# Router logits as plain float32 products on four column groups, scale tables right behind the token indices, and one filter unit moved out of the head

## The chip, the cores and the metric

The kernel is one launch on one core of a Trainium2 chip. A core has TensorE (matrix products and transposes), VectorE, ScalarE, GpSimd and SyncE (which issues most DMAs); the profile calls them PE, DVE, ACT, POOL and SP, and PE's loading of stationary operands is listed apart as PEld. The metric is device time in microseconds (us), the median of three runs.

## The reference

The output is `x + A(xn) + B(xn)` with `x = A_q` (2048 tokens x 512 channels, float32) and `xn` its layer norm.

- `A`: a 4-tap causal filter of `A_k` over time, times `A_v`; then a causal convolution over all 2048 steps with one filter per channel (`A_ssm_k`), plus a skip term `A_ssm_D`, times `xn`.
- `B`: a mixture of experts. `logits = xn @ w_gate` (512 x 8); each token takes its two best experts; the gates are the softmax of the two logits; expert e computes `silu(xn @ w1[e]) @ w2[e]` (512 to 1792 to 512), and the weighted results are summed.

```python
logits = xf @ w_gate
topk_idx = jnp.argsort(-logits, axis=-1)[:, :K]
topk_val = jnp.take_along_axis(logits, topk_idx, axis=-1)
gates = _softmax(topk_val, axis=-1)
```

## The kernel before

Products that must be exact use float32 values cut into a rounded part (a 4-byte format that TensorE reads in one pass, `F32R`) and a low part, in three products: rounded by rounded, rounded by low, low by rounded. A plain float32 product takes two passes, and the trace has two records for it.

The **head** runs before the first expert. `load_x` loads the tokens (eight tiles, 16 rows of tokens per partition in all), a table of constants and the filters `ks`. `logits` takes the tokens in four chunks of 512. For each chunk and each of four slices of 128 channels (`dc`) TensorE transposes four blocks into a PSUM tile `pt` (L253), ScalarE writes the rounded part `xTh` (L254), VectorE the low part `xTl` (L255). Eight products with the 16 columns of `wgr` (8 rounded, 8 low columns of the gate weights less their mean) add up in `pl` (L259). ScalarE copies `pl` to `lt` (L262), four small transposes bring it token by token into `pb` (L265), and VectorE adds the two halves to `lgt` (L271, L272). The mean and variance of the tokens (`stats`, L280) are put between, held back by explicit order.

`routing` finds each token's two best experts on VectorE (L353 to L365), counts tokens per expert and gives every token its place by products with triangular tables (L369 to L374), ranks the experts by load, and builds for the largest expert a one-hot table `tabA` (L552). Sixteen products with it (L433) give the list of that expert's tokens; VectorE turns it into indices `gix` (L580), and GpSimd gathers the tokens with six indirect DMAs (L885). `perm`, the experts in order of load, tells SyncE which weights to load (L974, L937). Another sixteen products with the same table (L571) give each gathered token its two scale values for the layer norm; `scales` copies them (L473), and VectorE normalizes the gathered tokens (L924). They are transposed (L905), cut into `xh` and `xl` (L909, L910), and the first expert's products start (L963): first those of the first three blocks of tokens (`u` = 0), then those of the other three.

**Filter units.** The long convolution goes through a two-step transform; its first step on the filters is `conv_k(pair, q8)`, eight units. A unit is eight transposes (L708), a copy by ScalarE (`kt`, L711), four float32 products of 512 columns, two on each half of TensorE's rows (L645), four copies from PSUM (L653, in one unit two of them on VectorE, L651) and two writes to DRAM (L673). PSUM has four banks for these products, the same four that the transposes of tokens use. Five units, (0,0) to (0,3) and (1,0), run in the head, as filling for TensorE; three run as background work between the first expert's products, as all other work on the convolution does between those of the experts.

The order on each engine comes from a list scheduler; `self.after(late, early, ...)` binds one instruction behind another, and `step` puts a unit's transposes or products behind the last instruction of its chain, `gate_t`. Six products of no use (`pads`, L428) stand ahead of the list.

## Time and profile before

| | us |
|---|---|
| median of three runs | 866.47 |
| lowest, highest | 865.88, 872.0 |
| the profiled execution | 868.49 |
| its span, first to last instruction | 866.7 |
| TensorE busy in the span | 837.3 |

The profiled execution takes 1.8 us more than its span, and 2.0 us more than the median. The profile gives, for each engine, its busy time; a table by stretches of the span with the granted share of TensorE's clock (1.00 is 2.4 GHz, 0.50 is 1.2 GHz); a list of instructions in order of time, in which neighbours of the same line are merged; and groups of instructions with their mean durations. Records of TensorE overlap, since a product starts before the one ahead has left the array.

### The profile page before, as it was taken

How to read it: one execution, taken by the hardware profiler on the slowest of the kernel's cores; microseconds unless marked ns; L12 is line 12 of the kernel's file. 1: busy time of each engine (PE TensorE's matmuls, PEld its weight loads, DVE VectorE, ACT ScalarE, POOL GpSimd, SP SyncE). 2: the span in 40 equal slices, each digit the busy share in tenths (PEclk: the TensorE clock that was granted, in tenths of full speed). 3: DMA queues.
4: the chain of work that ended last, by engine and by line, in shares of the span. 5: the costliest groups of instructions: out<-in, count | busy, mean ns of one | idle time of the engine just before them, and what ended most of it. 6: DMA issues, size and time to landing. Idle time of an engine off the chain costs nothing. (4 is left out here: it accounts for less than half of the span.)

```text
span 866.7 us, 13867 instructions
## 1 busy us (share of the span) xinstructions
PE 837.3 (97%) x5052; PEld 733.4 (85%) x5052; DVE 598.7 (69%) x878; ACT 499.3 (58%) x783; POOL 173.9 (20%) x168
## 2 busy tenths in 40 slices
PE   9889999999999989999999899999999989999996
PEld 7569998998998989998999788887888868888885
DVE  6869754679888746577766688658766489985421
ACT  4567425355433555567776678557875479654420
POOL 0110022460403402033020160105001220003231
PEclk9999999999999999999999999999999999999999
DMA  9599749969999675667465676656744599877971
GB/s 343 183 290 357 276 128 269 259 199 233 232 274 250 189 221 168 192 195 214 152 210 183 203 229 200 184 180 231 238 151 144 170 327 286 248 232 229 273 205 66
DMA packets 147506, 190.98 MB, mean 220 GB/s; under 512 B 12785, under 2 KB 106347, under 8 KB 146860
## 3 DMA queue, kind: packets, MB, share of 16 engines
q1 hardware_dynamic: 131356, 147.29, 56.7%
q0 software_dynamic: 16080, 42.78, 17.0%
q8 instruction: 41, 0.67, 0.3%
q14 instruction: 29, 0.24, 0.1%
HBM read 143.88 MB, written 50.63 MB: 224 GB/s over the span
## 5 line engine op out<-in xcount | busy, mean ns | idle before, releaser
L950 DVE TENSOR_TENSOR wl<-wraw,wh 128x1024 fp32r<-128x1024 f32 (+1 forms) x116 | 137.5, 1185 | 115.4 <-ACT wh L947 99.4
L947 ACT ACTIVATE wh<-wraw 128x1024 fp32r<-128x1024 f32 (+1 forms) x116 | 119.4, 1029 | 154.8 <-PE ps L963 103.4
L963 PE MATMUL ps<-xh,wh 128*128 128x512 f32 (+4 forms) x672 | 184.8, 327 | 9.9 <-ACT ht L1001 6.9
L963 PE MATMUL ps<-xl,wh 128*128 128x512 f32 (+4 forms) x672 | 184.0, 325 | 0.0
L963 PE MATMUL ps<-xh,wl 128*128 128x512 f32 (+4 forms) x672 | 183.3, 324 | 0.0
L963 PE MATMUL ps<-h,wh 128*128 128x288 f32 (+3 forms) x896 | 154.8, 292 | 2.5 <-ACT ht L1001 2.5
L963 PEld LDWEIGHTS ps<-xh,wh 128*128 128x128 f32 x672 | 113.6, 189 | 25.7 <-ACT ht L1001 10.0
L963 PEld LDWEIGHTS ps<-h,wh 128*128 128x128 f32 x896 | 129.5, 190 | 6.8 <-issue 3.0
L963 PEld LDWEIGHTS ps<-xl,wh 128*128 128x128 f32 x672 | 114.1, 189 | 9.8 <-issue 0.8
L963 PEld LDWEIGHTS ps<-xh,wl 128*128 128x128 f32 x672 | 114.1, 189 | 9.2
L1000 ACT ACTIVATE h<-ps 128x512 fp32r<-128x512 f32 (+4 forms) x112 | 67.9, 606 | 56.7 <-PE ps L963 56.5
L1002 DVE TENSOR_TENSOR h<-ht,h 128x512 fp32r<-128x512 f32 (+4 forms) x112 | 78.5, 705 | 27.2 <-ACT ht L1001 25.7
L963 PE MATMUL ps<-h,wl 128*128 128x288 f32 (+3 forms) x448 | 95.3, 292 | 0.0
L1032 POOL DMA_INDIRECT acc_d<-acc,ids x36 | 48.6, 1351 | 195.4 <-DVE acc L1029 187.5
L1051 PE MATMUL py<-wl,h 128*128 128x512 f32 x224 | 87.7, 391 | 0.0
L1052 PE MATMUL py<-wh,h 128*128 128x512 f32 x224 | 87.5, 391 | 0.0
L1050 PE MATMUL py<-wh,h 128*128 128x512 f32 x224 | 86.8, 391 | 0.0
L963 PEld LDWEIGHTS ps<-h,wl 128*128 128x128 f32 x448 | 72.0, 191 | 1.9 <-issue 1.5
L1001 ACT ACTIVATE ht<-ps 128x512 f32<-128x512 f32 (+4 forms) x112 | 68.1, 610 | 1.3 <-PE pty L1096 1.3
L1016 POOL DMA_INDIRECT acc<-acc_d,gix x36 | 46.7, 1297 | 86.9 <-PE ptx L905 52.1
L885 POOL DMA_INDIRECT xg<-xn_d,gix x34 | 39.7, 1167 | 114.2 <-DVE tb L581 55.4
L814 DVE TENSOR_TENSOR ka<-pu,ka 128x512 f32<-128x512 f32 x32 | 22.1, 692 | 40.8 <-ACT ka L808 37.1
(238 smaller groups left out, 1226.0 us busy)
## 6 DMA issues: line engine op xcount, KB each, us to landing
wraw<-in_B_w_dram SPq DMA_DIRECT2D x84, 512.0 KB
wraw<-in_B_w_dram SPq DMA_DIRECT2D x32, 448.0 KB
zk_d<-ev SPq DMA_DIRECT2D x16, 512.0 KB
zv_d<-ev SPq DMA_DIRECT2D x16, 512.0 KB
mid<-in_c_mid_dram POOLq DMA_DIRECT2D x16, 512.0 KB
z<-zk_d SPq DMA_DIRECT2D x32, 256.0 KB
z<-zv_d SPq DMA_DIRECT2D x32, 256.0 KB
zi_d<-zo SPq DMA_DIRECT2D x32, 256.0 KB
```

The costliest lines, as they stand in the source:

```text
L885: self.gather = nc.gpsimd.indirect_dma_start(out=t[:sb], out_offset=None, in_=self.xn_d[:, :] if r else self.io["A_q"].rearrange("o s d -> ...
L947: w = nc.scalar.activation(hi, raw, AF.Copy)
L950: t = nc.vector.tensor_sub(lo, raw, hi)
L963: self.mm = nc.tensor.matmul(ps[:, u, :n], w, x[:, u, :], start=first and w is wh and k == 0, stop=last and w is wl)
L1000: nc.scalar.activation(h, ps[:, :nu, :n], AF.Silu)
L1001: acts.append(nc.scalar.activation(t, ps[:, :nu, :n], AF.Silu))
L1002: self.hid = nc.vector.tensor_sub(l, t, h)
L1016: nc.gpsimd.indirect_dma_start(out=acc[:sb], out_offset=None, in_=sum_d[:, :], in_offset=bass.IndirectOffsetOnAxis(ap=self.gix[:sb, c0 + b ...
L1032: st = nc.gpsimd.indirect_dma_start(out=sum_d[:, :], out_offset=bass.IndirectOffsetOnAxis(ap=self.ids[:sb, c0 + b:c0 + b + 1], axis=0), in ...
L1050: nc.tensor.matmul(o, a, wh[:, f, :], start=ff == 0, stop=False)
L1051: nc.tensor.matmul(o, a, wl[:, f, :], start=False, stop=False)
L1052: nc.tensor.matmul(o, l, wh[:, f, :], start=False, stop=ff == FC - 1)
```

## The change

- **Logits.** The transposed tokens stay float32 (`xT`), with one copy by ScalarE; `xTl` and VectorE's subtractions are gone. Each slice of 128 channels has its own group of 32 of the array's columns (`pl[dc * Q:...]`, L257), with the gate weights padded to 32 columns by zeros: four float32 products per chunk, each into its own 32 partitions of `pl`, none added to another. ScalarE copies all 128 partitions to `lt` (L259), and a product with `pick`, a 0/1 matrix, adds the four groups and turns the result token by token into `pb` (L262). VectorE reads the logits straight from PSUM.
- **Statistics.** They follow each chunk, and the reciprocal deviations with them; on VectorE all 16 stand ahead of the first maximum (L343), and the steps from variance to the cut scales too. The load of ScalarE's table for SiLU moves behind the logits.
- **Routing.** The products of the scale tables (L558) stand right behind the list's (L423), their operands ahead of the indices on VectorE; `perm` and the copy of the places (`pos`) come behind the indices instead of ahead.
- **Units.** Four in the head, (0,0) to (0,3); (1,0) joins the background work of the first expert. All copies of the head's units are on ScalarE. The loads of both filter pairs are issued at the start, with a part of the constant table (`rc`) and of the transform (`ev`) between them.

```diff
         nc.sync.dma_start(rt, io["c_rt"][:, :cut])
-        nc.sync.dma_start(rc, io["c_rt"][:, cut:])
+        self.dv = self.cp.tile([P, DC], F32, name="dv")
+        nc.sync.dma_start(self.dv, io["A_ssm_D"].rearrange("(c p) -> p c", p=P))
...
+        self.ks = [self.load_k(cp, 0)]
         nc.sync.dma_start(self.ev, io["c_edge"][:, :P])
+        nc.sync.dma_start(rc, io["c_rt"][:, cut:])
+        self.ks.append(self.load_k(cp, 1))
...
-        wc = sp.tile([P, DC, E], F32, name="wc")
-        wg = sp.tile([P, DC, 2, E], F32R, name="wgr")
+        wc = sp.tile([P, DC, Q], F32, name="wc")
+        nc.gpsimd.memset(wc, 0.0)
         for dc in range(DC):
-            V.tensor_sub(wc[:, dc, :], self.wg[:, dc, :], pb[:, 1, :E])
-        V.tensor_copy(wg[:, :, 0, :], wc)
-        V.tensor_sub(wg[:, :, 1, :], wc, wg[:, :, 0, :])
-        self.L = sp.tile([P, NI, E], F32, name="lgt")
-        lp = sp.tile([P, NI, E], F32, name="lgp", tag="tmp")
+            V.tensor_sub(wc[:, dc, :E], self.wg[:, dc, :], pb[:, 1, :E])
+        pick = sp.tile([P, E], F32, name="pick")
+        V.tensor_reduce(pick, self.ident.rearrange("p (g q) -> p q g", q=Q)[:, :E, :], axis=AX.X, op=ALU.add)
...
         for c in range(4):
             x = self.x[4 * c:4 * c + 4]
-            xh = bp.tile([P, DC, D], F32R, tag="big", name="xTh")
...
+            xt = bp.tile([P, DC, D], F32, tag="big", name="xT")
             for dc in range(DC):
...
-                evict = nc.scalar.activation(xh[:, dc, :], pt, AF.Copy)
-                self.low[c, dc] = V.tensor_sub(xl[dc], pt, xh[:, dc, :])
+                nc.scalar.activation(xt[:, dc, :], pt, AF.Copy)
             pl = self.pmm.tile([P, 2, D], F32, tag="mm", name="pl")
-            for k, xt in enumerate(([xh[:, dc, :] for dc in range(DC)], xl)):
-                for dc in range(DC):
-                    nc.tensor.matmul(pl[:2 * E, 0, :], wg[:, dc].rearrange("p a e -> p (a e)"), xt[dc],
-                                     start=k == 0 and dc == 0, stop=k == 1 and dc == DC - 1)
...
-            lt = cp.tile([P, 4, DH], F32, tag="b4", name="lt")[:2 * E].rearrange("p a b -> p (a b)")[:, :D]
-            evict = nc.scalar.activation(lt, pl[:2 * E, 0, :], AF.Copy)
+            for dc in range(DC):
+                nc.tensor.matmul(pl[dc * Q:(dc + 1) * Q, 0, :], wc[:, dc, :], xt[:, dc, :], start=True, stop=True)
+            lt = cp.tile([P, 4, DH], F32, tag="b4", name="lt").rearrange("p a b -> p (a b)")[:, :D]
+            self.evict = nc.scalar.activation(lt, pl[:, 0, :], AF.Copy)
...
-                nc.tensor.transpose(pb[:, 0, 2 * jj * E:2 * (jj + 1) * E], lt[:, j * P:(j + 1) * P],
-                                    self.ident[:2 * E, :2 * E])
-            if c == 2:
-                self.stats(0)
-                self.stats(1)
-        pv = pb[:, 0, :2 * NI * E].rearrange("p (j a e) -> p j a e", j=NI, a=2)
-        V.tensor_copy(lp, pv[:, :, 1, :])
-        V.tensor_add(self.L, pv[:, :, 0, :], lp)
-        self.evict = evict
-        self.stats(2)
+                nc.tensor.matmul(pb[:, 0, jj * E:(jj + 1) * E], lt[:, j * P:(j + 1) * P], pick, start=True, stop=True)
+            self.stats(c)
+        self.L = pb[:, 0, :NI * E].rearrange("p (j e) -> p j e", j=NI)
+        self.rstds(sp)
...
-        self.stats(3)
         rs = sp.tile([P, 2, NI], F32, name="rs")
-        self.after(V.tensor_scalar_add(rs[:, 0, :], mv[:, :, 1], 1e-5), self.ranked, "the routing comes first")
-        self.rooted = nc.scalar.activation(self.rstd, rs[:, 0, :], AF.Sqrt)
-        self.after(self.rooted, self.evict, "the logits come first")
-        self.after(V.reciprocal(self.rstd, self.rstd), self.indexed, "the routing comes first")
+        V.tensor_scalar_add(rs[:, 0, :], mv[:, :, 1], 1e-5)
...
+        t = nc.scalar.activation(self.warm, self.warm, AF.Silu)
+        self.after(t, rooted, "the square root comes first")
+        self.after(t, self.evict, "the logits come first")
+        self.silu = t
...
+        step((0, 1))
+        step((0, 0))
         step((0, 2), held=self.held)
-        step((0, 1))
-        step((0, 3), held=self.held)
...
-        self.listed = self.gate_t = t
-        step((0, 2))
-        step((1, 0), shared=True, held=self.held)
-        step((0, 3))
-        self.ev03 = self.evicted
...
-        pv = sp.tile([1, E], F32, name="pv")
-        w9 = sp.tile([1, E, E], F32, name="w9")
-        V.tensor_mul(w9, ro[:1].rearrange("p e r -> p r e"), b1(rt["e0"])[:1])
-        V.tensor_reduce(pv, w9, axis=AX.X, op=ALU.add)
-        V.tensor_copy(self.perm, pv)
-        pos = t3("pos")
-        self.after(V.tensor_copy(pos.rearrange("p j e -> p (j e)"), pp[:, :P]), self.rtid, "the table comes first")
-
         tid0 = sp.tile([P, NBLK[0]], F32, name="tid0")
         self.indexed = self.unpack_tid(pt0, tid0[w], 0, NBLK[0], w)
         self.gathers(0)
-        self.rstds(sp)
+        pv = sp.tile([1, E], F32, name="pv")
+        w9 = sp.tile([1, E, E], F32, name="w9")
+        self.after(V.tensor_mul(w9, ro[:1].rearrange("p e r -> p r e"), b1(rt["e0"])[:1]), self.indexed,
+                   "the indices come first")
+        V.tensor_reduce(pv, w9, axis=AX.X, op=ALU.add)
+        ranks = V.tensor_copy(self.perm, pv)
+        pos = t3("pos")
+        self.after(V.tensor_copy(pos.rearrange("p j e -> p (j e)"), pp[:, :P]), ranks, "the ranks come first")
...
-        done = self.products(A0, B0, R1, parts, pt1, self.gate_t)
+        self.products(A0, B0, R1, parts, pt1, self.listed)
+        self.gate_t = self.tabled
+        step((0, 1))
+        step((0, 3), held=self.held)
+        step((0, 2))
+        self.ev02 = self.evicted
+        step((0, 3))
...
-        self.gate_t = self.tabled
-        step((1, 0))
...
-        if q8 == 0:
-            self.ks = self.load_k(cp, pair)
-        ks = self.ks
+        ks = self.ks[pair]
...
-            for q8 in range(2):
-                self.heads[0, q8] = self.conv_k(cp, 0, q8, True)
-                next(self.heads[0, q8])
-            for _ in self.heads[0, 0]:
-                pass
+            self.heads[0, 0] = self.conv_k(cp, 0, 0, True)
+            next(self.heads[0, 0])
...
-            units += [("k", lambda q8=q8: self.conv_k(cp, 1, q8)) for q8 in (1, 2, 3)]
+            units += [("k", lambda q8=q8: self.conv_k(cp, 1, q8)) for q8 in range(4)]
```

Three places in TensorE's own list of instructions, before and now (every row is an instruction or a run of equal ones; x16 is sixteen). Line numbers are those of the two files.

The first chunk of logits. Before:

```order
L253 MATMUL pt<-ident,x 128x128 x16
L259 MATMUL pl<-xTh,wgr 16x512 x2
L253 MATMUL pt<-ident,x 128x128 x4
L259 MATMUL pl<-xTh,wgr 16x512
L253 MATMUL pt<-ident,x 128x128 x4
L259 MATMUL pl<-xTh,wgr 16x512
L259 MATMUL pl<-xTl,wgr 16x512 x3
L253 MATMUL pt<-ident,x 128x128 x4
L259 MATMUL pl<-xTl,wgr 16x512
L253 MATMUL pt<-ident,x 128x128 x12
```

Now:

```order
L253 MATMUL pt<-ident,x 128x128 x16
L257 MATMUL pl<-xT,wc 32x512
L253 MATMUL pt<-ident,x 128x128 x4
L257 MATMUL pl<-xT,wc 32x512
L253 MATMUL pt<-ident,x 128x128 x4
L257 MATMUL pl<-xT,wc 32x512
L253 MATMUL pt<-ident,x 128x128 x4
L257 MATMUL pl<-xT,wc 32x512
L253 MATMUL pt<-ident,x 128x128 x16
L262 MATMUL pb<-pick,lt 128x8 x4
```

Four runs of the second chunk's transposes stood between eight products before; now they stand between four, so that each of the first chunk's products has transposes on both sides, where later chunks have four in a row.

From the last logits to the counts (`sel` marks the chosen experts, `ks` the filters). Before:

```order
L265 MATMUL pb<-ident,lt 128x16 x4
L708 MATMUL ptk<-ident,ks 128x128 x16
L645 MATMUL ps_397<-kt,ev 128x512
L645 MATMUL ps_396<-kt,ev 128x512
L645 MATMUL ps_403<-kt,ev 128x512
L645 MATMUL ps_402<-kt,ev 128x512
L369 MATMUL pw<-rt,sel 128x128
L372 MATMUL pw<-sel,rt 128x128
L373 MATMUL pw<-rt,cs 128x128
L374 MATMUL pw<-rt,cs 128x8
```

Now:

```order
L262 MATMUL pb<-pick,lt 128x8 x4
L690 MATMUL ptk<-ident,ks 128x128 x8
L359 MATMUL pw<-rt,sel 128x128
L362 MATMUL pw<-sel,rt 128x128
L363 MATMUL pw<-rt,cs 128x128
L364 MATMUL pw<-rt,cs 128x8
L690 MATMUL ptk<-ident,ks 128x128 x8
```

Eight transposes and the four products of unit (0,0) stood between the last logits and the first product that needs `sel`; now there are eight transposes alone, and (0,0)'s products come behind the counts.

The list, the scale tables (`tabR` with 24 columns) and the units. Before:

```order
L428 MATMUL pw<-ones 128x128 x6
L433 MATMUL pw<-tabR,tabA 96x6 x16
L645 MATMUL ps_538<-kt,ev 128x512
L645 MATMUL ps_537<-kt,ev 128x512
L645 MATMUL ps_544<-kt,ev 128x512
L645 MATMUL ps_543<-kt,ev 128x512
L708 MATMUL ptk<-ident,ks 128x128 x8
L645 MATMUL ps_570<-kt,ev 128x512
L645 MATMUL ps_569<-kt,ev 128x512
L645 MATMUL ps_576<-kt,ev 128x512
L645 MATMUL ps_575<-kt,ev 128x512
L571 MATMUL pw<-tabR_638,tabA 96x24 x16
```

Now:

```order
L418 MATMUL pw<-ones 128x128 x6
L423 MATMUL pw<-tabR,tabA 96x6 x16
L558 MATMUL pw<-tabR_524,tabA 96x24 x16
L632 MATMUL ps_548<-kt,ev 128x512
L632 MATMUL ps_547<-kt,ev 128x512
L632 MATMUL ps_554<-kt,ev 128x512
L632 MATMUL ps_553<-kt,ev 128x512
L690 MATMUL ptk<-ident,ks 128x128 x8
L632 MATMUL ps_575<-kt,ev 128x512
L632 MATMUL ps_574<-kt,ev 128x512
L632 MATMUL ps_581<-kt,ev 128x512
L632 MATMUL ps_580<-kt,ev 128x512
```

The scale tables' sixteen products moved from behind two units to right behind the list's. Behind the rows shown follow one more unit's four products and the transposes of the gathered tokens.

## Rows read from the trace of the kernel before

**Rows 1.** The page: the span; busy time of an engine, its share of the span, its instructions.

```profile
span 866.7 us, 13867 instructions
...
PE 837.3 (97%) x5052; PEld 733.4 (85%) x5052; DVE 598.7 (69%) x878; ACT 499.3 (58%) x783; POOL 173.9 (20%) x168
```

**Rows 2.** The table by stretches: start and end, length, then busy time (and instructions) of PE, PEld, DVE, ACT and POOL, TensorE's granted clock, mean share of the DMA engines, GB/s.

```profile
47.30:51.40 4.10, 2.38 (x9) 0.97 (x8) 2.52 (x9) 2.39 (x4) 0.20 (x2) 1.00 0.52 126
...
54.00:58.80 4.80, 4.80 (x28) 4.80 (x26) 3.60 (x7) 1.63 (x3) 0.00 (x0) 0.64 1.12 346
...
100.00:857.00 757.00, 743.50 (x4444) 654.50 (x4443) 516.48 (x639) 441.23 (x687) 163.23 (x145) 1.00 0.73 212
```

**Rows 3.** Instructions of PE in order of time (start, time to the end of the last one, engine, line, operation, tiles, shapes, count, and in brackets idle time ahead and what ended it): a product with 128 stationary columns and 8 moving ones, products of the logits, the last transposes of logits, and the products of unit (0,0).

```profile
3.00 1.71 PE L232 MATMUL pb<-wg,ones 128*128 128x8 f32 x8
...
18.99 1.10 PE L259 MATMUL pl<-xTh,wgr 128*16 128x512 f32 x4
...
19.93 0.85 PE L259 MATMUL pl<-xTl,wgr 128*16 128x512 f32 x3
...
25.42 0.42 PE L265 MATMUL pb<-ident,lt 16*128 16x16 f32 x4 [0.68 <-ACT lt L262]
...
29.14 1.99 PE L645 MATMUL ps<-kt,ev 64*128 64x512 f32 x8
```

**Rows 4.** Groups of instructions from 62 us on (busy time, mean ns of one record, idle time ahead): the three filter units among the first expert's products.

```profile
L645 PE MATMUL ps<-kt,ev 64*128 64x512 f32 x24 | 6.0, 615 | 0.0
...
L708 PE MATMUL ptk<-ident,ks 128*128 128x128 f32 x24 | 3.1, 274 | 0.0
```

**Rows 5.** Instructions of DVE in order of time: statistics, the first maximum, the copy of the places, the indices.

```profile
23.44 3.06 DVE L280 BATCH_NORM_STATS2 st<-x 128x6 f32<-128x512 f32 x5
...
27.25 0.29 DVE L353 TENSOR_REDUCE m<-lgt 128x16 f32<-128x128 f32 x1
...
39.51 0.29 DVE L449 COPY pos<-pw 128x128 f32<-128x128 f32 x1 [0.39 <-PE pw L433]
...
39.72 0.15 DVE L580 TENSOR_SCALAR gix<-pw 96x6 int32<-96x6 f32 x1
```

**Rows 6.** Instructions of PE in order of time, from the logits to the list.

```profile
25.77 1.16 PE L708 MATMUL ptk<-ident,ks 128*128 128x128 f32 x8
...
31.15 0.49 PE L369 MATMUL pw<-rt,sel 128*128 128x128 f32 x2
...
32.02 0.49 PE L372 MATMUL pw<-sel,rt 128*128 128x128 f32 x2 [0.38 <-DVE cs L371]
...
32.35 0.39 PE L373 MATMUL pw<-rt,cs 128*128 128x128 f32 x2
...
32.57 0.29 PE L374 MATMUL pw<-rt,cs 128*128 128x8 f32 x2
...
32.72 1.13 PE L708 MATMUL ptk<-ident,ks 128*128 128x128 f32 x8
...
37.95 1.52 PE L433 MATMUL pw<-tabR,tabA 128*96 128x6 f32 x16
```

**Rows 7.** Instructions of DVE in order of time: the copy of the scale tables, the first three blocks of gathered tokens, the second slice of weights, the low parts of the other three blocks.

```profile
48.97 0.17 DVE L473 COPY tb<-pw 96x24 f32<-96x24 f32 x1
...
50.77 1.45 DVE L924 TENSOR_SCALAR xg<-xg,sc,sc 96x512 f32<-96x512 f32 x3
...
56.53 1.21 DVE L950 TENSOR_TENSOR wl<-wraw,wh 128x1024 fp32r<-128x1024 f32 x1
...
60.14 1.55 DVE L910 TENSOR_TENSOR xl<-ptx,xh 128x288 fp32r<-128x288 f32 x4 [2.40 <-ACT xh L909]
```

**Rows 8.** Instructions of ACT in order of time: copies of a unit's products, the copy of its transposes, the first slice of weights, the first gathered tokens.

```profile
30.31 2.06 ACT L653 ACTIVATE ev<-ps 128x512 f32<-128x512 f32 x4
...
36.95 1.02 ACT L711 ACTIVATE kt<-ptk 128x1024 f32<-128x1024 f32 x1
...
46.98 1.04 ACT L947 ACTIVATE wh<-wraw 128x1024 fp32r<-128x1024 f32 x1
...
52.61 0.41 ACT L909 ACTIVATE xh<-ptx 128x288 fp32r<-128x288 f32 x1 [2.30 <-PE ptx L905]
```

**Rows 9.** Instructions of PE in order of time: the last unit's products, the first expert's first product, the transposes that follow the first 24 products, and two products at the full clock, seven apart.

```profile
47.30 2.37 PE L645 MATMUL ps<-kt,ev 64*128 64x512 f32 x8
...
53.97 0.51 PE L963 MATMUL ps<-xh,wh 128*128 128x288 f32 x2
...
58.76 1.16 PE L905 MATMUL ptx<-ident,xg 96*128 96x96 f32 x12
...
61.03 0.30 PE L963 MATMUL ps<-xh,wh 128*128 128x288 f32 x1
...
61.96 0.29 PE L963 MATMUL ps<-xl,wh 128*128 128x288 f32 x1
```

**Rows 10.** Instructions of POOL in order of time: the third gather, and the write that stands behind the last.

```profile
42.81 0.92 POOL L885 DMA_INDIRECT xg<-in_A_q_dram,gix  x1 [0.30 <-issue]
...
47.41 0.09 POOL L936 MEMSET wraw<- 1x1 f32 x1
```

**Rows 11.** DMA issues on SP in order of time: the first and the second slice of weights.

```profile
40.49 0.40 SPq L937 DMA_DIRECT2D wraw<-in_B_w_dram  x1
...
48.68 0.38 SPq L937 DMA_DIRECT2D wraw<-in_B_w_dram  x1
```

More of the change, by code (lines that the diff above doesn't have):

```diff
@@ L279, in stats @@
         for j in range(4):
[L280 to L283 removed]
+            V.bn_stats(st[:, j, :], self.x[4 * c + j])
         for j in range(4):
```

24 lines of the change are left out of this document (8 added, 16 removed).

## The prediction

> **What bounds the kernel now.** I read the page first: TensorE is busy 837.3 of 866.7 us [rows 1]. The table by stretches tells where the rest is: from 100 to 857 us its records cover 743.5 of 757.0, while between 47.3 and 51.4, shortly before the first expert, they cover 2.38 of 4.10 [rows 2]. So there are two regimes. Behind some 62 us a change pays what it adds to TensorE or takes from it; in the head a chain across engines decides, and I followed it in the lists by time. TensorE ends the logits at 25.84 [rows 3]; VectorE, still in statistics until 26.5, then copies and adds the halves (L271, L272) and takes the first maximum only at 27.25 [rows 5]; the chosen experts reach TensorE at 31.15, the counts end at 32.86, the list starts at 37.95 [rows 6], the indices at 39.72 [rows 5]. The third gather is issued at 42.81 [rows 10]. The scale tables are copied at 48.97 (their products stand behind two units), and three blocks are normalized at 50.77 [rows 7]; behind transposes and `xh` (52.61) [rows 8] the first expert starts at 53.97 [rows 9]. There the scale tables are last: the tokens were gathered before VectorE had them.
>
> **The sum**, edit by edit, as the shift of the point named.
>
> 1. *Logits.* A product of the old kind costs 0.235 (four from 18.99 to 19.93), so eight cost 1.88 a chunk [rows 3]. A float32 product of 512 columns takes two records. Unit (0,0)'s eight records take 1.99 on two halves of the rows, so a half's two products take 1.99 and one at most 1.0 [rows 3]; the two records of 128 columns from 32.35 to 32.57 take 0.11 each, or 0.44 for 512 columns, so one product 0.88 [rows 6]. I take 0.92. No row has products on column groups. Bounds for four: 0.92 if together, 3.7 if in turn. I take together, because the nearest row, two groups of rows, does so. In the first chunk transposes stand between them, so four cost 3.7 against 1.88: +1.8; three chunks give 3 x (0.92 - 1.88) = -2.9. The Trainium skill ("TensorE: Matmul & The Clock Gate", Part 3: Packing small matmuls) has three column tiles at a speedup of 2.38, not 3; by it four would take about 1.16, an estimate, and the sum would be 0.7 higher; no run here shows it. The product with `pick` has 128 stationary and 8 moving columns: between 0.15 (32.57 to 32.72) [rows 6] and 0.43 (1.71 / 4) [rows 3]; I take 0.2, near the later row, since it runs at the same clock. Four are 0.8 a chunk against 0.35 now (25.42 to 25.77): +1.8. Together +0.7 of TensorE's time, some of it in waits that are there anyway: logits end at 26.4, +0.6.
> 2. *To the chosen experts.* VectorE has no low parts to make, so its statistics and the reciprocal deviations are over before 26.4, and copy and addition are gone: maximum at 26.55 instead of 27.25, -0.7. One small operation (L442) joins the chain, +0.1. `sel` at 30.55, -0.6.
> 3. *Clock.* Now TensorE has one run of transposes and no product from 26.4 to 30.6, 4.2 us. In the rows the clock fell once: between the end of a unit's products at 49.67 (47.30 + 2.37) and 53.97 there were only transposes, 4.3 us, and the stretch 54.0 to 58.8 shows 0.64, between its two levels of 1.2 and 2.4 GHz [rows 2, 9]. So the likeliest is that it falls here too: the counts' 0.49 + 0.84 = 1.33 us of TensorE [rows 6] nearly double, +1.1, and work behind them loses 0.4. Bounds: 0 and +2.5.
> 4. *List and indices.* Between counts and list stand the same pieces as before (32.72 to 37.95) [rows 6], so the list starts at 38.85 (-0.6 + 1.5); the copy of places no longer stands ahead (39.51, then 39.72) [rows 5]: indices at 40.45, +0.7.
> 5. *Scale tables and tokens.* The tables' sixteen products follow at once and are as many (1.52 [rows 6]); begun with the list's end at 40.3, they end near 41.8 instead of being copied at 48.97. The gathers, +0.7, put the third at 43.5; its tokens were in place by 50.77 at the latest [rows 7], which bounds them at 51.5. I take them as there in time: the wait at 50.77 went to the tables. No longer last: the tables. Late next: ScalarE.
> 6. *ScalarE.* Units (0,1), (0,2), (0,3) now follow the tables, and all copies are its own. From 29.14 a unit's first copy came 1.17 later [rows 3, 8], so copies begin at 42.8. Twelve at 2.06 / 4, one copy of transposes 1.02 and the first weights 1.04 make 8.2: free at 51.0; the transposes of tokens wait for the last banks beside it; `xh` 0.41 [rows 8]: first expert at 51.45, -2.5.
> 7. *First 24 products.* Through this stretch ScalarE's copies end near 50, and TensorE's unit products, which refill the banks that they free, not long before, so the clock stays. 24 x 0.133 (seven from 61.03 to 61.96) + 0.4 = 3.6 against 58.76 - 53.97 = 4.8 [rows 9]: end at 55.05, -3.7.
> 8. *Weights.* `perm` behind the indices moves the first issue from 40.49 to 42.8 [rows 11]. They were cut from 46.98 [rows 8], so at 49.3 at the latest they are there, before ScalarE comes to them. The second issue at 48.68 [rows 11] stands behind SP's seven other reads of `perm` and GpSimd's write at 47.41 [rows 10]: between 0 and +2.3, I take 1.5. Its low part on VectorE, 1.21 from 56.53, precedes the other three blocks' low parts (60.14) [rows 7]; so not all of 3.7 is kept: the head ends -3.2 (bounds -2.3, -3.7).
> 9. *Unit (1,0).* Three units there cost 6.0 + 3.1 us of TensorE [rows 4]: one is +3.0, in full, as nothing there waits.
>
> Priced at nothing: SP's new order of `ks`, `rc`, `ev` (`ks` first needed at 25.77 [rows 6], `rc` just before the list); the clearing of `wc` on GpSimd, done during the load of the tokens; the write `k` behind the gathers.
>
> -3.2 + 3.0 = -0.2. The profiled execution took 868.49, 1.8 around its span, and 2.0 more than the median; against the median 866.47 the forecast is **866.2 us**.
>
> **Rivals.**
> - *The clock holds over the top-two search* (transposes at 25.8 bridge it). For: 25.84 to 29.14 held 3.3 us with transposes alone [rows 3]. The list comes 1.5 earlier and everything with it: 864.7.
> - *The clock falls again before the first expert*, as now: the last unit product ends early and ScalarE's 2 us of copies follow. That gives back step 7's 1.2: 867.4.
> - *Column groups pair off*: four in 1.84; the three later chunks cost 2.8 more: 869.0.
> - *Column groups run in turn* (slower). Place: L257, chunks 1 to 3; price 3.7 instead of 0.92, 3 x 2.8 = 8.3: 874.5. It decides the sign once a set takes over 1.0. The Trainium skill (same page and section) says that a load of stationary values passes running products only if its group of rows differs, and here all four use the same rows; by it this rival would hold. Against it: loads are busy 85% beside products at 97% in this trace [rows 1], on the same rows, so they do overlap.
> - *The change doesn't do what it says* in chunk 0, where transposes part the four; that is priced above.
>
> **Numbers.** Forecast 0.42, clock holds 0.22, second fall 0.12, pairs 0.12, in turn 0.08, others 0.04. The range takes the first four with the bounds of steps 3 and 8: 862.2 to 870.0; it leaves out the serial case and half the others. Runs of this kernel spread by some 6 us (865.88 to 872.0), so 1% is about what can be told from no change: 857.8 to 875.1. Faster needs more than twice the head's gain, 0.02; slower the serial case with another loss, 0.03; within 1%, 0.95.
>
> **What would show it.** Four records of L257 that overlap within about 1 us in chunks 1 to 3, 3.7 in chunk 0; L343 at 26.55; a granted share under 1.00 between 28 and 36; L423 and L558 side by side, the copy L462 near 42; ScalarE without gaps from 42.8 to 51; first L945 near 51.5 at the full clock; (1,0)'s products among the first expert's with some 3 us. I am wrong if sets take over 1.2, if tokens land after 51, or if the head's end moves by less than 2 us.

## The result, and the profile after

The changed kernel takes **873.56 us** (median of 20 runs, 871.41 to 878.44) against 867.49 for the kernel before (20 runs beside them, 865.76 to 872.0): ratio 1.0071 [1.0057, 1.0085], 6.1 us slower. The forecast was 866.2, the range 862.2 to 870.0. The profiled execution took 873.31.

The page of the changed kernel, as [rows 1]:

```profile
span 871.5 us, 13882 instructions
...
PE 845.2 (97%) x5068; PEld 737.6 (85%) x5068; DVE 586.4 (67%) x857; ACT 500.8 (57%) x786; POOL 173.0 (20%) x169
```

TensorE's busy time grew by 7.9 us although the logits need fewer products. Its table by stretches, columns as [rows 2], tells where: TensorE ran at half clock in two stretches of the head and in part of a third, 180 to 185. This is not of one execution alone: the mean granted clock is 0.983 to 0.989 in all 20.

```profile
18.00:26.60 8.60, 7.70 (x64) 4.82 (x64) 1.54 (x10) 4.85 (x11) 0.61 (x3) 1.00 0.86 355
26.60:37.00 10.40, 7.83 (x34) 6.78 (x36) 5.74 (x24) 2.92 (x5) 0.19 (x1) 0.51 0.00 0
37.00:43.70 6.70, 5.58 (x47) 4.31 (x43) 5.08 (x26) 3.62 (x6) 0.85 (x1) 1.00 0.52 154
43.70:50.50 6.80, 6.80 (x28) 4.24 (x28) 2.65 (x15) 1.78 (x4) 4.96 (x7) 0.50 0.77 225
...
180.00:185.00 5.00, 4.69 (x25) 4.69 (x26) 3.26 (x4) 1.41 (x3) 1.67 (x2) 0.66 0.93 329
```

TensorE of the changed kernel in order of time, as [rows 3, 6, 9]; last, the loading of stationary operands (PEld) for one set of four products:

```profile
9.79 1.05 PE L257 MATMUL pl<-xT,wc 128*32 128x512 f32 x2
...
17.26 0.96 PE L262 MATMUL pb<-pick,lt 128*128 128x8 f32 x8
18.15 1.06 PE L257 MATMUL pl<-xT,wc 128*32 128x512 f32 x8
...
24.63 1.07 PE L257 MATMUL pl<-xT,wc 128*32 128x512 f32 x8
26.44 1.75 PE L262 MATMUL pb<-pick,lt 128*128 128x8 f32 x8 [0.74 <-ACT lt L259]
28.04 1.95 PE L690 MATMUL ptk<-ident,ks 128*128 128x128 f32 x8
32.18 0.76 PE L359 MATMUL pw<-rt,sel 128*128 128x128 f32 x2 [2.19 <-ACT gt L443]
...
40.83 1.52 PE L423 MATMUL pw<-tabR,tabA 128*96 128x6 f32 x16
43.47 2.58 PE L558 MATMUL pw<-tabR,tabA 128*96 128x24 f32 x16 [1.11 <-DVE pos L439]
45.99 3.79 PE L632 MATMUL ps<-kt,ev 64*128 64x512 f32 x8
...
57.69 0.53 PE L945 MATMUL ps<-xh,wh 128*128 128x288 f32 x2
```

```profile
18.15 0.16 PEld L257 LDWEIGHTS pl<-xT,wc 128*32 128x32 f32 x8
```

One product of the first chunk takes 1.05 by itself (two records); four take 1.06 together (eight records), so the column groups do run at the same time. All eight loads are over 0.16 us after the first began, while the products run on to 19.21. Four products with `pick` take about 0.9. Behind the last set of logits TensorE waits 0.74 for ScalarE's copy, the clock falls at 26.6, and the same products with `pick` take 1.75 instead of 0.96, the transposes behind them 1.95 instead of 1.16 [rows 6]. The list starts at 40.83 (37.95 before), the scale tables at 43.47, each product at half speed; the first expert at 57.69 (53.97 before).

VectorE, then ScalarE, as [rows 5, 7, 8]:

```profile
28.23 0.29 DVE L343 TENSOR_REDUCE m<-pb 128x16 f32<-128x128 f32 x1 [5.45 <-PE pb L262]
...
43.14 0.27 DVE L439 COPY pos<-pw 128x128 f32<-128x128 f32 x1
...
46.18 0.17 DVE L462 COPY tb<-pw 96x24 f32<-96x24 f32 x1
...
49.94 1.00 DVE L906 TENSOR_SCALAR xg<-xg,sc,sc 96x512 f32<-96x512 f32 x2 [2.56 <-DMA xg<-in_A_q_dram,gix]
```

```profile
48.14 1.08 ACT L640 ACTIVATE ev<-ps 128x512 f32<-128x512 f32 x2 [7.32 <-issue]
...
54.75 2.58 ACT L640 ACTIVATE ev<-ps 128x512 f32<-128x512 f32 x5
57.13 1.11 ACT L891 ACTIVATE xh<-ptx 128x288 fp32r<-128x288 f32 x3
```

VectorE has the tables at 46.18 and, behind a wait of 2.56 us for the gathered tokens, normalizes the second and third block from 49.94 to 50.94. But ScalarE ends the copies of the three units only at 57.33, because it waits 7.32 us for the first unit's products: they stand behind the tables (43.47) and run at half clock. So neither the tables' copy nor the tokens are last any longer; ScalarE's copies are, at 57, not at 51.

A second loss stands where the second expert begins. TensorE, ScalarE and GpSimd of the changed kernel there:

```profile
176.59 0.50 PE L945 MATMUL ps<-xh,wl 128*128 128x276 f32 x2
...
180.31 0.83 PE L945 MATMUL ps<-xh,wh 128*128 128x276 f32 x2 [3.23 <-issue]
```

```profile
178.69 1.06 ACT L929 ACTIVATE wh<-wraw 128x1024 fp32r<-128x1024 f32 x1 [4.85 <-remote]
```

```profile
164.06 1.53 POOL L998 DMA_INDIRECT acc<-acc_d,gix  x1 [25.09 <-PE ptx L887]
...
172.84 0.95 POOL L867 DMA_INDIRECT xg<-xn_d,gix  x1 [0.30 <-PE pty L1078]
174.09 0.97 POOL L1014 DMA_INDIRECT acc_d<-acc,ids  x1 [0.30 <-DVE acc L1011]
```

TensorE waits 3.23 us (before: 0.97 at 172.89) and its clock falls behind it. ScalarE's copy of weights, which only waits for TensorE to be done with a buffer, starts at 178.69, 1.6 us after TensorE's last record (177.09). GpSimd meanwhile issues eleven indirect transfers with pauses of 0.3 us (164.06 to 179.99). Before, it rested 3.53 us ahead of its first scatter at 169.63. The first transfer of this row waits for a buffer that transposes (`ptx`) free. Four units instead of three now stand ahead of them among the first expert's products (the last from 150.6 to 156.5); with the later head they make the row start 6.4 us later (157.70 before), the scatters only 4.5, and the pause is closed.

Against the kernel before, TensorE is 2.2 us late when it begins the tables of the other experts (82.77, 80.59 before), 5.2 before the wait and 8.9 behind it. From there the profiles no longer differ by the change alone: the profiled execution of before waits 2.48 us at 321, where ScalarE stood 5.63 us behind a transfer, and its clock falls there. The one of after has neither; 4.7 is left behind that place, 4.8 in the spans.

### The profile page after: what moved, and what is told of

It is laid out like the page before. It is cut to its first block, busy times and chain, and to the rows that moved or that the text cites. A ratio compares the mean times of both kernels' runs of the same rounds, so it can differ in the third digit from the quotient of the medians.

```text
span 871.5 us, 13882 instructions
## 1 busy us (share of the span) xinstructions
PE 845.2 (97%) x5068; PEld 737.6 (85%) x5068; DVE 586.4 (67%) x857; ACT 500.8 (57%) x786; POOL 173.0 (20%) x169
## 5 line engine op out<-in xcount | busy, mean ns | idle before, releaser
L1014 POOL DMA_INDIRECT acc_d<-acc,ids x36 | 45.9, 1274 | 191.1 <-DVE acc L1011 183.5
L867 POOL DMA_INDIRECT xg<-xn_d,gix x34 | 42.3, 1245 | 116.3 <-DVE tb L568 55.4
L640 ACT ACTIVATE ev<-ps 128x512 f32<-128x512 f32 x64 | 33.2, 609 | 29.3 <-PE ps L632 20.1
```

The source lines that it names most:

```text
L867: self.gather = nc.gpsimd.indirect_dma_start(out=t[:sb], out_offset=None, in_=self.xn_d[:, :] if r else self.io["A_q"].rearrange("o s d -> ...
L1014: st = nc.gpsimd.indirect_dma_start(out=sum_d[:, :], out_offset=bass.IndirectOffsetOnAxis(ap=self.ids[:sb, c0 + b:c0 + b + 1], axis=0), in ...
```

## The experiments

Times are ratios to the kernel before in runs on the same chip; the marks are those of one profiled execution. "First" is the start of the first expert, "tables" that of the other experts' tables, "wait" the one before the second expert's first products.

| run | ratio | first | tables | wait |
|---|---|---|---|---|
| before | 1 | 53.97 | 80.59 | 0.97 |
| the change | 1.0071 [1.0057, 1.0085] | 57.69 | 82.77 | 3.23 |
| b_logits | 1.0028 [1.0009, 1.0046] | 61.26 | 87.36 | 0.97 |
| b_unit | 1.0052 [1.0035, 1.0070] | 54.41 | 80.95 | 4.81 |
| b_log_pads | 0.9981 [0.9965, 0.9997] | 53.88 | 79.82 | 0.97 |
| a_pads | 1.0051 [1.0030, 1.0072] | 54.81 | 80.17 | 4.91 |
| a_pos | 1.0091 [1.0066, 1.0117] | 57.63 | 82.98 | 4.73 |
| b_unit_late | 1.0099 [1.0077, 1.0121] | 54.36 | 80.92 | 0.97 |
| a_late | 1.0463 [1.0436, 1.0491] | 52.20 | 77.52 | 0.97 |
| a_g3 | 1.0023 [1.0003, 1.0043] | 52.73 | 78.55 | 0.97 |
| a_g3_pos | 1.0049 [1.0030, 1.0068] | 54.88 | 80.22 | 4.98 |
| b_g3 | 1.0037 [1.0023, 1.0050] | 52.12 | 82.82 | 0.98 |
| b_log_pads_g3 | 0.9994 [0.9976, 1.0012] | 54.08 | 86.03 | 0.98 |
| b_unit_g3 | 1.0050 [1.0033, 1.0067] | 51.63 | 82.98 | 4.87 |
| a_run | 1.0229 [1.0186, 1.0272] | 57.09 | 82.19 | 0.97 |
| b_run | 1.0089 [1.0053, 1.0126] | 54.15 | 80.43 | 0.98 |
| a_run2 | 1.0055 [1.0034, 1.0076] | 56.51 | 81.61 | 0.97 |
| a_pads_run2 | 1.0008 [0.9990, 1.0027] | 52.66 | 78.00 | 0.97 |
| a_pads_run | 1.0130 [1.0104, 1.0156] | 54.73 | 80.07 | 0.97 |
| b_log_pads_run | 1.0143 [1.0115, 1.0170] | 56.14 | 83.31 | 0.97 |

**Parts of the change alone.** b_logits is the kernel before with the new logits and statistics (L233 to L268 of the changed kernel) and nothing else; b_unit has the unit's move alone:

```diff
-        step((1, 0), shared=True, held=self.held)
...
-        step((1, 0))
...
-            units += [("k", lambda q8=q8: self.conv_k(cp, 1, q8)) for q8 in (1, 2, 3)]
+            units += [("k", lambda q8=q8: self.conv_k(cp, 1, q8)) for q8 in range(4)]
```

> The kernel before with the new logits alone (four column groups, the product with the 0/1 matrix, statistics behind each chunk); units, tables and routing as before. Theory A (the clock's fall at 26.6 us in the changed kernel comes from the logits themselves, which keep TensorE in products for 1.06 us a chunk where the old ones took about 2): the clock falls at 26 to 27 us here too, although unit (0,0)'s products stand behind the logits again; the counts start near 34 instead of 31.15 and the time is +2 to +3.5 us. Theory B (the fall comes from unit (0,0)'s products missing behind the logits): the clock holds up to the counts, the last logits end near 27.3 instead of 25.84, the counts start at 31.1 to 31.5, and the time is 0 to +0.8 us.

> The kernel before with one part of the change alone: unit (1,0) leaves the head and joins the first expert's background work. Theory (a unit costs its TensorE time in full among the experts' products): +3.0 us from expert 0's second half on, by the trace; the head gets shorter, since the scale tables stand behind one unit less, by 1 to 2.5 us; so +0.5 to +2.0 against the kernel before. Rival (the change's loss of 6 us is this unit, through what its transfers and copies disturb later): +5 us or more. Rival (hidden there as in the head): 0 or below.

In b_logits the clock falls at 26.6 and stays low to 37, as in the changed kernel, though unit (0,0) stands behind the logits there. So it is the new logits, not the order of units behind them, that lose it. b_unit's head costs 0.4, its unit 3.1 of TensorE; but the wait before the second expert grows from 0.97 to 4.81 and the clock falls behind it. The move costs more than the unit's products.

**The clock held by useless products.** b_log_pads is b_logits with three products that nobody reads between the last chunk's logits and their copy; a_pads is the changed kernel with those and eleven more behind the last products with `pick`:

```diff
+            self.pads(last, (0, 0, 0, 3)[c])
             lt = cp.tile([P, 4, DH], F32, tag="b4", name="lt").rearrange("p a b -> p (a b)")[:, :D]
...
+        for _ in range(n):
+            t = self.nc.tensor.matmul(pt[:, :P], self.ones, self.ones, start=True, stop=True)
```

> b_logits with three useless products of 128 columns on TensorE between the last chunk's logits and the copy of them. Theory (what the new logits cost is the clock's fall at 26.6 us; with a little more work in the wait it holds over unit (0,0), whose own products then keep it): the counts start at 31.5 to 32.5 instead of 36.7, the first expert near 55 to 56 instead of 61.3, and the time is 0 to +1 us over the kernel before. Rival (the unit's place or the longer logits cost it, not the clock; or three products are too few): the counts stay near 36, +2 us.

> The changed kernel with 14 useless products of 128 columns on TensorE where it waits: three between the last chunk's logits and the copy of them, eleven behind the last product with the 0/1 matrix. Theory (the head's loss is the clock, 1.2 GHz from 26.6 to 37 us): the clock holds through the counts, these take 1.7 us instead of 2.6, the list starts 1.5 to 2.5 us earlier than 40.83, and the time is 1.5 to 3 us below the changed kernel (870.5 to 872 where it has 873.6), as the second fall at 43.7 stays. Rival (the clock falls at its own time, or the clock matters little because VectorE sets the head): the products run at half speed and delay the counts by about 2 us: +2 us above the changed kernel, or no difference.

Both hold the full clock past 40 us; then it falls for 3.4 us, at 52.9 in b_log_pads and at 42.5 in a_pads. In b_log_pads the ratio falls from 1.0028 to 0.9981, some 4 us, and it is under the kernel before, the only run whose whole interval is. In a_pads the same places read:

```profile
25.97 1.06 PE L263 MATMUL pb<-pick,lt 128*128 128x8 f32 x8
26.89 2.70 PE L273 MATMUL pad<-ones 128*128 128x128 f32 x22
...
37.80 1.52 PE L432 MATMUL pw<-tabR,tabA 128*96 128x6 f32 x16
40.44 1.53 PE L567 MATMUL pw<-tabR,tabA 128*96 128x24 f32 x16 [1.11 <-DVE pos L448]
```

The list is 3.0 us earlier than in the changed kernel and the first expert 2.9; the time gains 1.7 us (1.0071 to 1.0051), which the overlapping intervals don't tell from nothing. The wait before the second expert is still 4.91.

**The tables' wait for the copy of the places.** The first table product waits 1.11 us for VectorE's copy `pos`. Both use the PSUM tile `pw`. In a_pos the copy stands behind that of the tables:

```diff
         scales()
+        pos = t3("pos")
+        self.after(V.tensor_copy(pos.rearrange("p j e -> p (j e)"), pp[:, :P]), self.scaled, "the scales come first")
```

> The changed kernel with the copy of the places put behind the copy of the scale tables, so that the tables' first product waits for the indices and their flags, not for the places as well. Theory (that wait, 1.1 us by the trace, is on the path and opens the gap in which the clock falls a second time): the tables' products start 0.5 us earlier (42.95 for 43.47), the first expert's too, and the time is 0.5 us below the changed kernel if the clock still falls at 43.7, 2 to 3 us below if it holds. Rival (the tokens, normalized at 50.9 us, are last): no difference.

The tables come earlier (42.75), the first expert at 57.63 as before, and the ratio shows no gain. I took that for proof that the tables are not on the path. The profile does not bear that out. TensorE, then ScalarE:

```profile
47.20 1.66 PE L690 MATMUL ptk<-ident,ks 128*128 128x128 f32 x8
```

```profile
51.40 1.02 ACT L693 ACTIVATE kt<-ptk 128x1024 f32<-128x1024 f32 x1 [3.02 <-PE ps L632]
```

The transposes end at 48.86 and are copied 2.5 us later, so this execution lost at another place what the tables gained. What their wait costs stays open.

**The gathers in two runs.** In several heads ScalarE starts on finished transposes late. In a_pads those of the second unit end at 46.55, and `kt` is copied at 48.58. I suspected the run of six gathers and issued three of them later, behind the normalization of the first three blocks:

```diff
-        self.gathers(0)
+        self.gathers(0, range(3))
...
+            if u == 0:
+                gix = self.cp.tile([QM, NBLK[0]], I32, name="gix2", bufs=1)
+                i = nc.vector.tensor_copy(gix[:sb, :], self.gix[:sb, :NBLK[0]])
+                self.after(i, t, "the first half comes first")
...
+                self.gathers(0, range(3, 6), gix)
```

> The changed kernel with the useless products of a_pads, and with the second three gathers of tokens issued behind the normalization of the first three, not in one run with them. In the traces TensorE's work for the units is done up to 2 us before others see it (in a_pads the copy of the last transposes starts at 48.58 though they end at 46.55), each time 2.2 us after the last gather of the run began. Theory (TensorE's signals are held up while the run of gathers lasts): the copy of (0,3)'s transposes starts at most 0.3 us behind their end, ScalarE's last unit copy ends near 52 instead of 54.46, the first expert starts near 52.3 instead of 54.8; the second half of the tokens comes up to 2 us late, so that the time is 0 to 2 us below a_pads' 872.5. Rival (the delay has another cause, the transfers of the weights say): the copy starts 2 us late as before, and the second half costs some 2 us.

> The kernel before, with one thing moved: the first expert's second three gathers are issued on GpSimd behind the normalization of the first three tiles of tokens (from a copy of the indices made there), instead of all six in one run. Theory S (signals of finished TensorE work reach the other engines late while a run of gathers is being issued): the scale tables' copy, at 48.97 before though TensorE's last table product ended earlier, comes between 46 and 47.5, directly behind the products; the first expert's products begin between 52.0 and 53.0 (53.97 before), the ratio is 0.997 to 0.999. Rival (those signals are late for a cause that the number of gathers in a run does not touch): the copy stays at 48.5 to 49.2, the first expert at 53.5 to 54.5, and the ratio is 0.999 to 1.001, or over it, because the second half of the first expert's tokens now waits for its gathers.

> The changed kernel with useless products that hold the clock, the gathers in two runs of three, and the copy of the places put behind the copy of the scale tables. If the wait of the tables for that copy (about 1 us) is on the path now that the signals are not late, the first expert's products begin between 51.7 and 52.3 (52.73 with the gathers alone) and the ratio is 1.000 to 1.002. Rival (the third gather's landing sets the first expert's start, the tables do not): 52.6 to 52.9, ratio 1.002 to 1.003.

> The kernel before with the new logits, the three useless products before the last copy of the logits, and the gathers in two runs of three; unit (1,0) stays in the head. If what the gathers save (1.0051 to 1.0023 on the changed kernel with useless products) adds to what the logits save with the clock held (0.9981), the ratio is 0.994 to 0.997 and the table of positions begins between 77.5 and 79.0. Rival (in the kernel with unit (1,0) in the head the scale tables' copy was not late, 47.05, so the second three gathers only come later): ratio 0.997 to 1.001, first expert's products not before 53.5.

> The kernel before, with unit (1,0) in the background as in the changed kernel, and the gathers in two runs of three. Theory U (the unit itself, standing between the first expert and the second, makes the wait at the second expert's first products): the wait is 3 to 5 us as in the run with the unit alone (4.81), and the ratio is that run's 1.0052 less what the gathers save, 1.002 to 1.004. Theory T (the wait is a matter of when TensorE gets there against GpSimd's indirect transfers, so that it goes when the head is moved by some microseconds): the wait is 1.0 to 1.5 us, the clock does not fall there, and the ratio is 0.999 to 1.002.

a_g3 gained what was expected, and I took that for proof. The four runs that followed bear it out in part: in none of the five heads with two runs of gathers do the semaphore events show TensorE's work seen late. But their times do not improve with it. b_g3 has its tables and its first expert early (46.96, 52.12), but the second half of the tokens now comes late, and the ratio is 1.0037; b_log_pads_g3 waits 2.27 us for those tokens, its clock falls there, and its ratio is 0.9994, no better than b_log_pads. a_g3_pos differs from a_g3 by the place of one copy and has `kt` at 48.53, but not by a late signal: its transposes ended at 48.43, since its clock was low from 41.2 to 48.0. Last, a_pads_run and a_pads_run2 below have the head of a_pads, all six gathers in one run, in other executions: `kt` at 48.50 in the one, but right behind its transposes (46.21) in the other, whose first expert starts at 52.66 instead of 54.81. ScalarE in a_pads, then in a_pads_run2:

```profile
48.58 1.02 ACT L702 ACTIVATE kt<-ptk 128x1024 f32<-128x1024 f32 x1 [2.36 <-PE ps L641]
```

```profile
46.30 1.02 ACT L702 ACTIVATE kt<-ptk 128x1024 f32<-128x1024 f32 x1
```

So a run of six goes along with late signals in some executions and not in others, and a_g3's gain may be such a draw.

a_g3 and a_g3_pos also show what happens before the second expert. TensorE and ScalarE of a_g3, then of a_g3_pos:

```profile
171.61 0.50 PE L963 MATMUL ps<-xl,wh 128*128 128x276 f32 x2
...
173.78 0.39 PE L963 MATMUL ps<-xh,wh 128*128 128x276 f32 x1 [0.97 <-ACT ht L1001]
```

```profile
172.15 1.06 ACT L947 ACTIVATE wh<-wraw 128x1024 fp32r<-128x1024 f32 x1 [2.60 <-PE ps L963]
```

```profile
173.29 0.50 PE L963 MATMUL ps<-xl,wh 128*128 128x276 f32 x2
...
179.46 0.83 PE L963 MATMUL ps<-xh,wh 128*128 128x276 f32 x2 [4.98 <-ACT ht L1001]
```

```profile
177.84 1.06 ACT L947 ACTIVATE wh<-wraw 128x1024 fp32r<-128x1024 f32 x1 [6.61 <-remote]
```

The same products end 1.68 us later in the second (173.79, 172.11). ScalarE's `wh`, which follows them, starts 0.04 after their end in a_g3 and 4.05 after it in a_g3_pos: the news that TensorE was done came 4 us late. In the trace's semaphore events five signals of products that ended from 173.53 to 174.48 arrive between 177.77 and 177.94, 2.5 us after GpSimd began the last of its ten transfers.

**The unit's place.** b_unit_late is b_unit with (1,0) behind the eight value-filter units; part of the filter's transform is then read before it is written. a_late is a_pads with that and the copy of a_pos.

> The kernel before with unit (1,0) in the background, but behind the value filter's eight units instead of ahead of them. Theory (the unit costs 3.1 us of TensorE's time wherever it lies, and another 3 to 5 us because it pushes what the second expert starts with into each other: TensorE's wait there is 0.97 us before, 3.2 to 4.9 us in each of three kernels with the unit ahead of them, and the clock falls behind it): the wait at the second expert's start is back at about 1 us, the unit's 3.1 us are still paid, later, and the time is +1.5 to +3.5 us over the kernel before, 1 to 3 us below b_unit's +4.0. Rival (the long wait comes with any shift of the program by some us): it stays, and the time is that of b_unit.

> The changed kernel with the useless products of a_pads, the places copied behind the scale tables, and unit (1,0) behind the value filter's units. Theory (the losses add: clock in the head 1 us and more, the wait at the second expert's start 3 to 5 us): 868 to 870, within 2.5 us of the kernel before, the rest being the unit's 3.1 us less what the head gains. Rival (the wait at the second expert's start is not the unit's): 871.5 to 873.

GpSimd rests 4.22 and 4.90 us ahead of its scatters and the wait before the second expert is 0.97 in both, but neither is faster. b_unit_late waits 3.15 us at 327, near where the kernel before waits 2.48; what else it pays wasn't followed. a_late, expected at 868 to 870, takes 903.65: it waits 8.19, 4.61, 4.86, 4.43 and 5.34 us between 219 and 343, most often for VectorE's `kva`, and its clock falls at each of these. Why it waits there was not followed.

**The order of GpSimd's transfers.** a_run issues each later expert's gathers behind the scatters of the expert before the last; a_run2 and a_pads_run2 do so for the third expert alone (`r == 2`):

```diff
+            if r > 1:
+                self.after(self.gather, self.scattered, "the sums of the expert before come first")
             self.xg.append(t)
...
+            self.scattered = st
```

> The changed kernel, with each later expert's gathers of tokens issued on GpSimd behind the scatters of the expert before the last one, instead of ahead of and between them; nothing is left out. Theory R (signals of finished TensorE work are held up while GpSimd issues indirect transfers back to back, and the unit in the background made that run long): the run before the second expert is six scatters at most, the wait before the second expert's first products is 1.0 to 1.5 us and the clock does not fall there, and the ratio falls from 1.0071 to 1.001 to 1.004. Rival 1 (the six scatters alone hold the signals up as well): the wait stays at 3 to 5 us, ratio 1.005 to 1.008. Rival 2 (the gathers now come too late for the third expert): a new wait before the third expert's transposes, ratio above 1.008.

> The kernel before with the order of GpSimd's transfers alone. Its wait at the second expert is 0.97 us already. If the order is worth something only where the unit in the background made the run long, the ratio is 0.998 to 1.001; if the order by itself spares stalls everywhere (the profiled execution of before has one of 2.48 us at 321), it is 0.994 to 0.998, and what it gives on the changed kernel cannot all be put to the change's account.

> The changed kernel, with the third expert's six gathers of tokens alone issued on GpSimd behind the first expert's scatters; the later experts' transfers stand as in the changed kernel. Theory R: the wait before the second expert's first products is about 1 us as in the run with the order changed for all experts, no long run comes into being later, and the ratio is the changed kernel's 1.0071 less 4.1 us, 1.0015 to 1.004. Rival (the time comes back later: the signals are held up behind another run, or the execution draws another stall): ratio 1.005 to 1.009 with a new wait of 3 us or more after 185 us.

> The same order on the changed kernel with the useless products that hold the clock in the head (1.0051 without the order). Theory R: wait about 1 us, ratio 0.999 to 1.002. Rival: ratio 1.004 to 1.007 with a new wait of 3 us or more after 185 us.

a_run's GpSimd rests 6.33 us between the gathers and the scatters, the wait before the second expert is 0.97 and the clock holds; but the ratio is 1.0229. The order put on the later experts makes a longer run there. GpSimd and ScalarE of a_run:

```profile
382.27 1.03 POOL L1016 DMA_INDIRECT acc_d<-acc,ids  x1 [8.84 <-DVE acc L1013]
...
401.80 0.98 POOL L1000 DMA_INDIRECT acc<-acc_d,gix  x1 [0.30 <-issue]
```

```profile
390.34 1.06 ACT L608 ACTIVATE hi<-z 128x1024 fp32r<-128x1024 f32 x1
405.18 0.61 ACT L984 ACTIVATE h<-ps 128x528 fp32r<-128x528 f32 x1 [13.78 <-remote]
```

Sixteen transfers with pauses of 0.3 us, and ScalarE waits 13.78 us for TensorE's signals, until 3.4 us after the last began; ScalarE's lag against the changed kernel grows by some 15 us between 385 and 409. b_run (1.0089) and the same order on b_log_pads (b_log_pads_run, 1.0143, expected at 0.993 to 0.998) lose 8 to 9 us at the same place. On a_pads (a_pads_run, expected at 0.999 to 1.002) it gives 1.0130, but the one execution of it that was profiled, of 869.0 us, goes through the same sixteen transfers without such a wait; its other four take 877 to 879, and six of b_run's seven 875.6 to 878.8, the seventh 867.6. So such a wait needs no unit in the background: a long run is enough, by the times in most executions.

With the third expert's gathers alone moved, GpSimd and TensorE of a_run2 read:

```profile
164.74 1.19 POOL L1000 DMA_INDIRECT acc<-acc_d,gix  x1 [0.30 <-issue]
172.26 0.96 POOL L1016 DMA_INDIRECT acc_d<-acc,ids  x1 [6.33 <-DVE acc L1013]
```

```profile
176.92 0.53 PE L947 MATMUL ps<-xh,wh 128*128 128x276 f32 x2 [0.97 <-ACT ht L985]
```

The wait is gone and no long one comes back later. a_pads_run2 falls from 1.0051 to 1.0008, 3.7 us, as theory R had it; a_run2 from 1.0071 to 1.0055, 1.4 us, less than expected and not clear of noise. Its clock is still lost in the head: 0.987 to 0.990 in its six executions, 0.993 to 0.997 in the twelve of a_pads_run2. What this order gives on the kernel before by itself was not run.

## Why the prediction was wrong

The sign was held at zero by a head of -3.2 and a unit of +3.0. The unit cost what was said; the head came out at +2.2 (the other experts' tables at 82.77 instead of 80.59), and behind the unit stood a wait that the sum had not. The verdict "within 1%" came out (+0.71%), but by its width, not by the sum: that was luck.

1. *Logits.* The prices held: four products in 1.06 against 0.92, a chunk's products with `pick` 0.9 against 0.8. At the full clock (a_pads) the logits ended at 27.03, +1.2 rather than +0.6; in the changed kernel at 28.19, by the clock. The rivals "pair off" and "in turn" fell. The Trainium skill ("TensorE: Matmul & The Clock Gate", Part 3: Packing small matmuls) says that a load overlaps running products only where the groups of rows differ. The trace does not agree: these four use the same rows, and the loads of the second passes start from 18.18 on, beside first passes that run from 18.15 to 18.79. Nor is the estimate of 1.16 from its speedup for three column tiles borne out, since four take what one takes.
2. *To the chosen experts.* The search took 3.85 us as before; it only began late (28.23 instead of 26.55).
3. *Clock: failed, in size.* I let it fall in the search, behind 26.4, for +1.5 (bounds 0 and +2.5). It fell at 26.6, right behind the wait of 0.74 for ScalarE, so the last `pick` products grew too (+0.8), besides the counts (+0.9) and what follows (+1.0): +2.7 to the list. And it fell again at 43.7, which no step had, for +1.1 in the tables and +1.0 to the first unit's first copy. I looked only at the stretch without products behind the logits, and not at the logits: the kernel before holds its clock across a wait of 0.68 at the same place, but its last chunk's products take 2.03 ahead of it (22.72 to 24.75), these 1.07; three useless products in the wait were enough to hold it (b_log_pads). In three other executions of this head (a_pos, a_run, a_run2) it fell at 27.9 to 29.5, and each time before the counts. Holding it was worth some 4 us on the kernel before with the logits alone (1.0028 to 0.9981).
4. *List and indices.* From the counts' end to the list 6.05 against 5.09 at half clock, where step 3 had +0.4; from the list to the indices 1.56 against 1.77, as said.
5. *Scale tables and tokens: failed.* "Follow at once" left out the PSUM tile that the tables share with the places: a wait of 1.11, and half clock, so 46.18 instead of 41.8. ScalarE's copies stand behind these tables (step 6), so this is on the path here.
6. *ScalarE: failed, where the misses add up.* I took ScalarE as busy without gaps from 42.8. Its copies begin at 48.14: the list is 2.0 late, the tables' wait adds 1.1, half clock the 2.1 of step 3. From there they take 9.2 instead of 8.2, as they wait on unit products at half clock: 57.33 instead of 51.0. With the clock held to 42, three executions with one and the same head give 54.46 (a_pads) and 54.38 (a_pads_run), with signals some 2 us late, and 52.30 (a_pads_run2) without.
7. *First 24 products.* The full clock came as said; from the first product to ScalarE's first `ht` it is 8.66 instead of 10.20, -1.5 against -1.2.
8. *Weights.* Not decisive; the head ended where step 6 put it.
9. *Unit (1,0): the price right, the claim wrong.* TensorE's lag grows by 3.0, from 2.2 to 5.2, where the fourth unit runs. But "in full, as nothing there waits" looked at TensorE alone. The unit also delays the transposes that free GpSimd's buffers, closes the pause in its transfers, and costs 2.3 us more of waiting at the second expert and 1.4 of clock.

Steps 5 and 6 also rest on a reading of the profile of before that was wrong: that the tables are copied at 48.97 is not for the two units ahead of them alone. TensorE, then VectorE's first reader of the tables, of the kernel before:

```profile
45.85 1.53 PE L571 MATMUL pw<-tabR,tabA 128*96 128x24 f32 x16
```

```profile
48.88 0.17 DVE L487 TENSOR_TENSOR ov<-pw,capv 128x8 f32<-128x8 f32 x1 [3.33 <-PE ps L645]
```

The products end at 47.38, 1.5 us before VectorE starts on them; in b_g3 and b_log_pads, where their place is the same, the copy comes at 46.96 and 47.05. So the wait that the sum took for the tables' place was for some 1.5 us a late signal, of the kind told in the last section.

The chances put 0.12 on a second fall of the clock, but priced it at 1.2. With both losses taken away (a_pads_run2) the change gives 1.0008 [0.9990, 1.0027]; the forecast was 0.9997. In its profile the other experts' tables come 2.6 earlier than before, where -3.2 was forecast, and TensorE is 0.4 late behind the unit.

## What to carry to other kernels

Fewer and shorter products on a bound engine can cost more than they save where they leave TensorE with pauses: look at what stands in the row between the last product and its next wait, and price the half clock for all that follows. When work is put among a bound engine's products, follow the buffers that the delayed work frees, to the queues that wait for them. A wait that shows in one profile should be looked for in other executions before an edit is credited with it.

## What was not expected of the hardware

While GpSimd issues indirect transfers with pauses of only 0.3 us, signals of finished TensorE work can reach the other engines microseconds late. In a_g3_pos (ten transfers), as in b_unit, a_pads and b_unit_g3, they come together, 2.4 to 2.5 us after the last transfer of the run began and some 4 us late; in a_run (sixteen) ScalarE waits 13.8 us, until 3.4 us after the last began. In the changed kernel and in a_pos they come one by one while the run goes on: five products that ended from 176.14 to 177.09 are told of between 177.24 and 181.50.

Whether a pause stands ahead of the scatters goes with it in all but one of the 20 profiles. In all thirteen where GpSimd rests 3.1 us or more ahead of the scatters, with the unit in the head or not, the wait before the second expert is 0.97 or 0.98. Of the seven without a pause, all with unit (1,0) ahead of the value filter's units, six wait 3.23 to 4.98 us, and a_g3, with the same transfers, 0.97. What holds the signals up, and why not in a_g3 or in the profile of a_pads_run, is open.
